# Top-k attention and a SoLU block on one Trainium2 core: the places of the work in a step are changed, and they rank work for a scheduler where they were the order on four engines

## The chip, the cores and the metric

One NeuronCore of a Trainium2 chip runs the whole program. Its engines run their own queues in order and wait for each other through semaphores: PE (TensorE, matmuls and transposes), DVE (VectorE), ACT (ScalarE), POOL (GpSimd), and SP, which here issues all DMA transfers. The metric is the device time of one execution in microseconds (us). Less is better.

## The reference, cut to what matters

```python
# q, k, v: (8, 8, 576, 64)  batch, heads, sequence, head size
scores = scale * q @ k.T                      # 576 x 576 for each head
kth = 32nd largest score of each row
attn = softmax of the row over the scores >= kth, 0 elsewhere
x = attn @ v                                  # as (4608 tokens, 512)
h = x @ w_in                                  # (4608, 1024)
solu = h * softmax(h)
ln = (solu - mean) / sqrt(var + 1e-6) * g_ln
out = ln @ w_out                              # (4608, 512)
```

The MoE weights w_in, w_out and g_ln arrive as 64-bit floats and are converted on the chip.

## The kernel before

The work is cut into 32 pairs (a batch and two of its heads, 9 row tiles of 128 x 576 scores each) and 36 token tiles of 128 tokens. A pair goes through these functions, in this order of dependence:

- `prep_t`, `prep_m`, `moments`, `spread` (PE, with ACT copies `prep_tc` L621, `prep_mc` L639 and L643, `moments_c` L660): transposes q and k, and works out a first guess of the 32nd largest score. `spread_v` (DVE, L690 and L693), `spread_r` (DVE, L701), `first_p` (POOL, L706 to L712) and `first` (DVE, L720) finish the guess.
- `scores` (PE, L745), `evac` (ACT, L756: PSUM to the tile X).
- three counts that narrow the threshold, each over the nine row tiles: `count0` (DVE, L764), then `second` (DVE, L772 to L779); `count1` (ACT, L787), then `third` (DVE, L796 to L804); `count2` (ACT, L819).
- `exps` (ACT, L851, three pieces of three row tiles), `side`, `nearest` (DVE, L840 and L844), `kth` (DVE, L857 to L872): the exact threshold; `keep` (DVE, L881) and `inverse` (L889, L892): masked exponentials and the reciprocal of their sum; `norm` (POOL, L896).
- `transpose_p`, `transpose_last` (PE, L907, L927), `copy_p`, `copy_last` (ACT), `attn_v` (PE, L956), `copy_v` (ACT, L966, L968).

A token tile goes through `mm1` (PE, L980), `hmax` (DVE, L989), `hexp` (ACT, L994), `solu` (DVE, L1004), `square` (ACT, L1014), `ln` (POOL, L1020 to L1025), `transpose_ln` (PE, L1032), `copy_ln` (ACT, L1039), `mm2` (PE, L1044) and `store` (ACT, L1051, then the DMA).

Every call of such a function is put on a list with a place, a number that counts from the step of its pair: `at(place, function, ...)`. A step is one pair, `STEP = 38.0`. `pair_times` gives the places of a pair, `token_times` those of a token tile, `batch_times` says in which steps the token tiles of a batch run: one in each step, and in three steps, where the last 64 positions of two batches are ready, two ("double" below). The list is sorted by place and the calls are made in that order. Before the change all this stands inside `manual_schedule` for PE, ACT, DVE and POOL: these engines run the instructions in the order of the calls. SP's queue was left to the scheduler.

Pools with a fixed number of buffers tie the engines together: two PSUM buffers `big` for y_ps, s_ps and h_ps, two `tp` for all transposes, two `o` for om, ot, o_ps and y_t; two SBUF buffers `lnT`, used for the raw weights (w_raw) as well; two `w`.

The 16 weight chunks are converted in three stages on DVE and POOL (`float64_stages`). `weights_step(n)`, four times in a step, opens chunk n and takes every open chunk one stage further.

Of the kernel before, what the change touches and what calls it, by code (L numbers as in the profile page):

```python
# [65 lines left out]
def general_path(  # L66
# [175 lines left out]
    def topk_softmax(i, t):  # L242
        d = st[i]
        d["P", t] = []
        for sb in d.pop(("S", t)):
            cur, e, m = sb, None, None
            for r in range(TOPK // 8):
                m = small.tile([P, 8], F32, tag="m8", name="m8")
                nc.vector.max(m, cur)
                if r == 0:  # L250
# [193 lines left out]
def fast_path(  # L444
# [30 lines left out]
    NP = H // 2  # L475
# [21 lines left out]
    NPAIR = len(pairs)  # L497
# [26 lines left out]
    w_chunks = []  # L524
# [49 lines left out]

# [480 lines left out]
    todo = []  # L1057
    STEP = 38.0

    def at(time, f, *args):  # L1060
        todo.append((time, len(todo), f, args))

    def pair_times(i):
        b = i * STEP
        at(b - 32, load_qk, i)
        at(b + 1, load_v, i)

        at(b - 17.0, prep_t, i)
        at(b - 16.4, prep_m, i, "q")
        at(b - 13.0, prep_tc, i)  # L1070
        at(b - 12.8, prep_mc, i, "q")
        at(b - 12.7, prep_m, i, "k")
        at(b - 12.2, prep_mc, i, "k")
        at(b - 12.1, moments, i)
        at(b - 11.7, moments_c, i)
        at(b - 11.5, spread, i)
        at(b - 10.5, spread_v, i)
        at(b - 9.7, spread_r, i)
        at(b - 9.0, first_p, i)
        at(b - 6.5, first, i)  # L1080

        for t in range(NM + 1):
            at(b - 9.0 + 1.8 * t, scores, i, t)
        for j in range(NT):
            at(b - 7.5 + 0.9 * j, evac, i, j)
            at(b - 2.0 + 0.77 * j, count0, i, j)
            at(b + 6.4 + 0.77 * j, count1, i, j)
            at(b + 17.7 + 0.77 * j + (1.5 if j > 3 else 0), count2, i, j)
        at(b + 5.2, second, i)
        at(b + 14.3, third, i)  # L1090

        b += STEP
        for g, t in enumerate((4.8, 14.6, 16.1)):
            at(b + t, exps, i, g)
            at(b + 6.2 + 4.26 * g, side, i, g)
            at(b + 30.2 + 2.25 * g, inverse, i, g)
        at(b + 23.0, kth, i)
        for j in range(NT):
            at(b + 6.3 + 1.42 * j, nearest, i, j)
            at(b + 27.9 + 0.75 * j, keep, i, j)  # L1100
            at(b + 31.2 + 0.9 * j, norm, i, j)
            at(b + 32.2 + 0.95 * j, transpose_p, i, j)
            at(b + 32.8 + 0.95 * j, copy_p, i, j)
        for part, t in enumerate((35.5, 39.2, 40.5)):
            at(b + t, transpose_last, i, part)
            at(b + t + 0.6, copy_last, i, part)
        for part, t in enumerate((36.8, 40.6, 42.4)):
            at(b + t, attn_v, i, part)
        at(b + 43.0, copy_v, i, 1)
        at(b + 43.8, copy_v, i, 2)  # L1110

    def token_times(n, x, stores, more=0.0):

        d = {"x": x, "stores": stores}
        late = n > NPAIR
        b = (NPAIR + 1) * STEP + 6.0 + 15.0 * (n - NPAIR - 1) if late else n * STEP + more
        at(b + 6.5, mm1, d)
        at(b + 14.0, hmax, d)
        at(b + 15.4, hexp, d)
        at(b + 17.5, solu, d)  # L1120
        at(b + 20.5, square, d)
        at(b + 22.0, ln, d)
        lt, c = (28.7, 30.0) if late else (27.2, STEP + 13.7 - more / 2)
        for g in range(2):
            at(b + lt + 0.3 * g, transpose_ln, d, g)
            at(b + lt + 0.6 + 0.4 * g, copy_ln, d, g)
        at(b + c, mm2, d)
        at(b + c + 7.3, store, d)

    def batch_times(b):  # L1130
        rows = out[b * S : b * S + SM, :].rearrange("(p t) m -> p t m", t=NM)
        n = NP * (b + 1) + 1
# [15 lines left out]

    at(-10.0, load_g)
    at(-14.0, load_w, 0)  # L1150
    for n in range(len(w_chunks) + 2):
        at(11.0 + STEP / 4 * n, weights_step, n)
    for i in range(NPAIR):
        pair_times(i)
    for b in range(B):
        batch_times(b)
    E = mybir.EngineType
    with tc.manual_schedule(engines={E.PE, E.Activation, E.DVE, E.Pool}):
        for _, _, f, args in sorted(todo, key=lambda x: x[:2]):
            f(*args)  # L1160

# [59 lines left out]
```

## Time and profile before

| | |
|---|---|
| runs | 1852.15, 1855.78, 1857.37 us (median 1855.78) |
| the profiled execution | 1855.06 us, its span 1853.2 us |
| PE busy | 1478.1 us (80%) |
| DVE busy | 1258.0 us (68%) |
| ACT busy | 1159.3 us (63%) |
| POOL busy | 554.0 us (30%) |
| TensorE clock granted, mean | 0.821 of full speed |

The span is the time from the first to the last instruction that the profile shows; the execution's own time is 1.9 us longer. No engine is busy all the time, so the busy shares alone do not tell what sets the end: that is read from the chain of waits and from the step. The granted clock has two levels, 1.2 GHz (0.50 in the rows) and 2.4 GHz (1.00).

### The profile page before, as it was taken

To read this page: it belongs to the slowest core of one execution; us is meant where nothing else is said; L and a number is where in the kernel's file an instruction comes from. 1 tells how busy PE (TensorE), PEld (TensorE's weight loads), DVE (VectorE), ACT (ScalarE), POOL (GpSimd) and SP (SyncE) were. 2 spreads that over 40 slices of the span, in tenths; PEclk is the share of its full clock that TensorE was granted. 3 is DMA by queue.
4 is the path that set the end of the run, shared out by engine and by line. 5 is a ranking of instruction groups with operands and counts; after the bars stand their busy time and mean duration, and the time that the engine had idled before them with its cause. 6 is when DMAs were issued, how large, how long until landed. Compare 5 with 4: busy or idle time off the path is not lost.

```text
span 1853.2 us, 21831 instructions
## 1 busy us (share of the span) xinstructions
PE 1478.1 (80%) x7043; PEld 822.0 (44%) x7043; DVE 1258.0 (68%) x2976; ACT 1159.3 (63%) x2398; POOL 554.0 (30%) x613
## 2 busy tenths in 40 slices
PE   5365357988888888888888897988888897888898
PEld 3132234544444444544444444444444454444443
DVE  3667677677777766677777776577777775777611
ACT  5544566666767775676777774677777764677422
POOL 3457542223333212233322222333222323322310
PEclk9665667788878897888888997888889977888899
DMA  2111100011001110101101000111110000100000
GB/s 72 56 48 47 54 23 16 20 26 26 20 27 26 27 26 7 30 21 26 26 26 27 26 14 20 25 26 26 27 27 19 20 20 20 32 13 13 7 12 25
DMA packets 101899, 48.70 MB, mean 26 GB/s; under 512 B 86920, under 2 KB 95120, under 8 KB 101776
## 3 DMA queue, kind: packets, MB, share of 16 engines
q1 hardware_dynamic: 101776, 47.21, 9.5%
q8 instruction: 59, 0.97, 0.2%
q14 instruction: 64, 0.52, 0.1%
HBM read 37.75 MB, written 9.44 MB: 25 GB/s over the span
## 4 chain that ended last, share of the span: by engine, by line
PE 48%; ACT 33%; DVE 11%; POOL 3%; DMA 2%; issue 2%; SPq 0%; DVEq 0%; ACTq 0%; POOLq 0%
PE s_ps L745 15%; ACT junka L787 8%; ACT sg L819 8%; PE om L956 8%; PE tp_p L907 7%; PE h_ps L980 6%; PE o_ps L1044 6%; ACT PT L921 4%; ACT E L851 3%; ACT X L756 3%; DVE E L881 3%; PE tp_pt L927 2%; DVE w L840 2%; DVE w L844 2%; PE tp_ln L1032 2%
## 5 line engine op out<-in xcount | busy, mean ns | idle before, releaser
L745 PE MATMUL s_ps<-qkT 64*128 64x288 f32 (+1 forms) x1280 | 384.4, 607 | 87.9 <-ACT X L756 55.6
L764 DVE TENSOR_SCALAR_CACHE_REDUCE junkv<-X,t 128x576 bf16<-128x576 f32 x288 | 222.9, 808 | 233.0 <-ACT X L756 232.2
L921 ACT COPY PT<-tp_p 128x512 f32<-128x512 f32 x256 | 147.4, 591 | 336.0 <-PE tp_p L907 336.0
L745 PEld LDWEIGHTS s_ps<-qkT 64*128 64x128 f32 (+1 forms) x1280 | 196.2, 255 | 233.0 <-ACT X L756 135.0
L896 POOL TENSOR_SCALAR E<-E,rden 128x576 f32<-128x576 f32 x288 | 272.6, 965 | 16.6 <-DVE rden L892 14.0
L756 ACT ACTIVATE X<-s_ps 128x576 f32<-128x576 f32 x288 | 186.1, 657 | 145.2 <-PE s_ps L745 111.9
L881 DVE SCALAR_TENSOR_TENSOR E<-X,kth,E 128x576 f32<-128x576 f32 x288 | 260.9, 937 | 0.2
L907 PE MATMUL tp_p<-ident,E 128*128 128x128 f32 x1152 | 219.8, 334 | 50.4 <-POOL E L896 35.9
L1044 PE MATMUL o_ps<-w_out,lnT 128*128 128x512 f32 x576 | 253.9, 594 | 1.2 <-ACT lnT L1039 1.2
L840 DVE SCALAR_TENSOR_TENSOR w<-X,al,sg 128x576 f32<-128x576 f32 x288 | 235.1, 816 | 3.4
L980 PE MATMUL h_ps<-w_in,xTm 128*128 128x512 f32 x512 | 228.0, 598 | 0.0
L819 ACT ACTIVATE sg<-X,t 128x576 bf16<-128x576 f32 x288 | 220.4, 773 | 9.6 <-DVE t L804 9.6
L844 DVE MAX8 w<-w 128x8 f32<-128x576 f32 x288 | 219.2, 761 | 9.9
L787 ACT ACTIVATE junka<-X,t 128x576 bf16<-128x576 f32 x288 | 219.1, 766 | 7.5 <-DVE al L828 5.1
L907 PEld LDWEIGHTS tp_p<-ident,E 128*128 128x128 f32 x1152 | 154.3, 168 | 143.8 <-POOL E L896 75.7
L812 POOL TENSOR_SCALAR tt<-t 128x9 f32<-128x9 f32 x32 | 7.0, 219 | 648.7 <-DVE al L828 646.1
L631 PE MATMUL tp_qk<-ident,km 128*128 128x128 f32 x128 | 32.5, 403 | 187.7 <-ACT qkT L621 187.7
L1044 PEld LDWEIGHTS o_ps<-w_out,lnT 128*128 128x128 f32 x576 | 108.8, 190 | 136.5 <-issue 129.9
L851 ACT ACTIVATE E<-X 128x1728 f32<-128x1728 f32 x96 | 156.9, 1639 | 0.0
L980 PEld LDWEIGHTS h_ps<-w_in,xTm 128*128 128x128 f32 x512 | 94.9, 190 | 110.5 <-issue 107.9
L956 PE MATMUL om<-PT,vm 128*64 128x256 f32 x1024 | 124.6, 385 | 0.0
L690 DVE TENSOR_TENSOR yq<-y_ps,qm 128x512 f32<-128x512 f32 x32 | 22.1, 691 | 140.2 <-PE y_ps L672 130.7
(114 smaller groups left out, 1681.7 us busy)
## 6 DMA issues: line engine op xcount, KB each, us to landing
qm<-in_q_dram SPq DMA_DIRECT2D x32, 256.0 KB, 3.4
km<-in_k_dram SPq DMA_DIRECT2D x32, 256.0 KB, 3.4
vm<-in_v_dram SPq DMA_DIRECT2D x32, 256.0 KB, 2.7
out_dram<-osb SPq DMA_DIRECT2D x32, 256.0 KB, 2.3
w_raw<-in_moe_w_in_dram SPq DMA_DIRECT2D x8, 512.0 KB, 3.9
w_raw<-in_moe_w_out_dram SPq DMA_DIRECT2D x8, 512.0 KB, 3.5
qt<-in_q_dram SPq DMA_DIRECT2D x32, 32.0 KB, 2.2
kt<-in_k_dram SPq DMA_DIRECT2D x32, 32.0 KB, 2.8
```

The source lines that it names most:

```text
L745: nc.tensor.matmul(out=s[:, half, 0:SH], lhsT=qkT[hd, 0, qs], rhs=qkT[hd, 1, half * SH : (half + 1) * SH], start=True, stop=True,)
L756: nc.scalar.activation(out=x_of(i, j).rearrange("p (a s) -> p a s", a=2), in_=d.pop(("s", j))[:, :, 0:SH], func=AF.Copy, scale=scale,)
L787: nc.scalar.activation(out=junk, in_=x_of(i, j), func=AF.Sign, scale=-1.0, bias=d["t1"][:, j : j + 1], accum_out=d["n1"][:, j : j + 1],)
L819: nc.scalar.activation(out=d["sg", j], in_=x_of(i, j), func=AF.Sign, scale=-(1.0 + 2.0**-23), bias=d["t2"][:, j : j + 1], accum_out=d["n2" ...
L840: nc.vector.scalar_tensor_tensor(out=w, in0=x_of(i, j), scalar=d["al"][:, j : j + 1], in1=d.pop(("sg", j)), op0=ALU.subtract, op1=ALU.mult,)
L844: nc.vector.max(d["w8"][:, j, :], w)
L881: nc.vector.scalar_tensor_tensor(out=e, in0=x_of(i, j), scalar=d["kth"][:, j : j + 1], in1=e, op0=ALU.is_ge, op1=ALU.mult, accum_out=den_a ...
L896: nc.gpsimd.tensor_scalar(out=e, in0=e, scalar1=st[i]["rden"][:, j : j + 1], scalar2=1.0, op0=ALU.mult, op1=ALU.mult,)
L907: nc.tensor.transpose(tp[:, c, :], p_of(i, j)[:, c * P : (c + 1) * P], ident)
L956: nc.tensor.matmul(out=o[h * D : (h + 1) * D, :], lhsT=vm[:, h, c, :] if c < NM else vt[:, h, :], rhs=rhs[0:ks, c, :], start=(c == 0), sto ...
L980: nc.tensor.matmul(out=h[:, half, :], lhsT=x[:, c, :], rhs=w_in[:, c, half * 512 : (half + 1) * 512], start=(c == 0), stop=(c == NP - 1),)
L1044: nc.tensor.matmul(out=d["o"], lhsT=d["lnT"][:, c, :], rhs=w_out[:, c, :], start=(c == 0), stop=(c == NF - 1),)
```

## The change

The functions compute what they did; the number of instructions on each engine is the same. Three things differ. The frame `manual_schedule` is gone: the list is still walked by place, but an instruction's place now only ranks it, and the scheduler that builds the program sets the order on PE, ACT, DVE and POOL too, instruction by instruction. The places are other numbers. And `weights_step(n)` is called three times for each chunk, so that a chunk's three stages have places 0, 5 and 7.5 behind its start, all ahead of the next chunk's (9.5 on). The token tiles of a batch run one step later against the pairs.

```diff
-    w_open = []
+    w_gen = [finish_w(n) for n in range(len(w_chunks))]
...
-        if n < len(w_chunks):
-            w_open.append(finish_w(n))
-        for g in list(w_open):
-            if next(g, w_open) is w_open:
-                w_open.remove(g)
+        next(w_gen[n], None)
...
-        for g, t in enumerate((4.8, 14.6, 16.1)):
+        for g, t in enumerate((12.0, 14.4, 19.5)):
             at(b + t, exps, i, g)
...
-            at(b + 27.9 + 0.75 * j, keep, i, j)
+            at(b + 25.5 + 0.75 * j, keep, i, j)
...
-        n = NP * (b + 1) + 1
+        n = NP * (b + 1) + 2
...
-    for n in range(len(w_chunks) + 2):
-        at(11.0 + STEP / 4 * n, weights_step, n)
+    for n in range(len(w_chunks)):
+        for t in (0.0, 5.0, 7.5):
+            at(10.0 + STEP / 4 * n + t, weights_step, n)
...
-    E = mybir.EngineType
-    with tc.manual_schedule(engines={E.PE, E.Activation, E.DVE, E.Pool}):
-        for _, _, f, args in sorted(todo, key=lambda x: x[:2]):
-            f(*args)
+    for _, _, f, args in sorted(todo, key=lambda x: x[:2]):
+        f(*args)
```

Three places in the middle of the program show what this makes of the order. Line numbers of the changed kernel are 4 lower. The first is ACT, from the end of a pair's transposes to the square of the token tile. Before (E is `exps`, junka `count1`, sg `count2`, h_ps and solu belong to the token tile):

```order
L851 ACTIVATE E<-X 128x1728
L966 COPY xTm<-om 128x512
L968 COPY xTt<-ot 128x64
L787 ACTIVATE junka,n_5886<-X,t_5884 128x576 x9
L851 ACTIVATE E<-X 128x1728
L994 ACTIVATE e_sb,rs<-h_ps,hmax 128x1024
L851 ACTIVATE E<-X 128x1728
L819 ACTIVATE sg,n_5887<-X,t_5959 128x576 x4
L1014 ACTIVATE e_sb,var<-solu,nmu 128x1024
L1051 COPY osb<-o_ps 128x512
L819 ACTIVATE sg,n_5887<-X,t_5959 128x576 x4
L621 COPY qkT<-tp_t 128x2x64
```

The same place on ACT in the change:

```order
L847 ACTIVATE E<-X 128x1728
L917 COPY PTt<-tp_p 128x512
L929 COPY PTt<-tp_pt 64x128
L783 ACTIVATE junka,n_6245<-X,t_6243 128x576 x5
L962 COPY xTm<-om 128x512
L783 ACTIVATE junka,n_6245<-X,t_6243 128x576
L964 COPY xTt<-ot 128x64
L783 ACTIVATE junka,n_6245<-X,t_6243 128x576 x3
L847 ACTIVATE E<-X 128x1728
L990 ACTIVATE e_sb,rs<-h_ps,hmax 128x1024
L815 ACTIVATE sg,n_6246<-X,t_6310 128x576 x5
L1010 ACTIVATE e_sb,var<-solu,nmu 128x1024
```

Two of the three E now stand ahead of the copies of the last transposes (the first of them five rows above the rows shown, between two PT copies), one stays in front of the token tile's exponential, and the copies of om and ot have moved in among the nine counts. Behind the last row come osb, the two qkT copies, one sg, the third qkT copy, one sg, the copy into mom and the last two sg. In the six steps at and after a double one all nine sg stand ahead of the qkT copies.

The second place is DVE, from the `keep` of one pair to the `nearest` of the next. Before (junkv is `count0`; r, u and t `second`; w and its maximum `nearest`):

```order
L881 SCALAR_TENSOR_TENSOR E,den_all<-X,kth,E 128x576 x2
L889 TENSOR_SCALAR rden<-den_all 128x3
L892 RECIPROCAL rden<-rden 128x3
L764 TENSOR_SCALAR junkv,c_6097<-X,t_6119 128x576 x9
L772 TENSOR_SCALAR r<-c_6097 128x9
L775 RECIPROCAL r<-r 128x9
L777 TENSOR_TENSOR u<-r,tb 128x9
L779 TENSOR_TENSOR t_6299<-u,ta 128x9
L828 SCALAR_TENSOR_TENSOR al<-n_5887,tt 128x3
L840 SCALAR_TENSOR_TENSOR w<-X,al,sg 128x576
```

In the change the same stretch of DVE begins with

```order
L716 TENSOR_TENSOR t_6087<-mean,zs 128x9
L836 SCALAR_TENSOR_TENSOR w<-X,al,sg 128x576
L718 SCALAR_TENSOR_TENSOR ta<-zs,t_6087 128x9
L760 TENSOR_SCALAR junkv,c_6048<-X,t_6087 128x576 x2
L840 MAX w_5886<-w 128x8
L760 TENSOR_SCALAR junkv,c_6048<-X,t_6087 128x576 x2
L836 SCALAR_TENSOR_TENSOR w<-X,al,sg 128x576 x2
L840 MAX w_5886<-w 128x8
L760 TENSOR_SCALAR junkv,c_6048<-X,t_6087 128x576 x2
```

The nine counts of a pair and the nine `nearest` of the pair before it now alternate; `kth` and six of the nine `keep` follow, ahead of the token tile's hmax, and three `keep` behind it. Before, nine `keep` stood ahead of the counts and all `nearest` behind them, three of these behind hmax.

The third place is POOL, around the token tile's `ln`. Before (E is `norm`; var, rstd and solu are `ln`):

```order
L712 TENSOR_SCALAR tb<-zs 128x9
L896 TENSOR_SCALAR E<-E,rden 128x576 x9
L812 TENSOR_SCALAR tt<-t_6374 128x9
L1020 TENSOR_SCALAR var<-var 128x1
L1024 TENSOR_TENSOR rstd<-var,mhalf 128x1
L1025 TENSOR_SCALAR solu<-solu,nmu,rstd 128x1024
```

In the change:

```order
L708 TENSOR_SCALAR tb<-zs 128x9
L892 TENSOR_SCALAR E<-E,rden 128x576 x6
L808 TENSOR_SCALAR tt<-t_6725 128x9
L892 TENSOR_SCALAR E<-E,rden 128x576 x3
L1016 TENSOR_SCALAR var<-var 128x1
L1020 TENSOR_TENSOR rstd<-var,mhalf 128x1
```

The `norm` of a pair are now cut in six and three, and the three stand directly ahead of `ln`; they belong to the pair whose `keep` has just run, and PE transposes their tiles in the step that follows. On PE the pieces in a step are the same ones, and half of `transpose_ln` (four of eight) now stands ahead of `spread`.

## Rows read from the trace of the kernel before

**Rows 1.** The page's first part, busy time of each engine.

```profile
PE 1478.1 (80%) x7043; PEld 822.0 (44%) x7043; DVE 1258.0 (68%) x2976; ACT 1159.3 (63%) x2398; POOL 554.0 (30%) x613
```

**Rows 2.** Timeline of DVE, `spread_r` of six of the 32 pairs: start, duration.

```profile
10.36 0.76 DVE L701 TENSOR_REDUCE ss<-yq 128x9 f32<-128x576 f32 x1
...
94.35 0.74 DVE L701 TENSOR_REDUCE ss<-yq 128x9 f32<-128x576 f32 x1
...
383.55 0.75 DVE L701 TENSOR_REDUCE ss<-yq 128x9 f32<-128x576 f32 x1
...
692.04 0.75 DVE L701 TENSOR_REDUCE ss<-yq 128x9 f32<-128x576 f32 x1
...
808.95 0.75 DVE L701 TENSOR_REDUCE ss<-yq 128x9 f32<-128x576 f32 x1
...
1658.96 0.75 DVE L701 TENSOR_REDUCE ss<-yq 128x9 f32<-128x576 f32 x1
```

**Rows 3.** Chain that ended last, in order of time, 888 to 942 us: start, length.

```profile
887.40 6.07 ACT junka L787 x16
893.47 1.54 ACT E L851
895.00 1.09 ACT e_sb L994 x2
...
900.66 1.13 ACT e_sb L1014 x2
...
907.51 0.42 PE y_ps L672 x8
...
928.33 1.47 PE s_ps L745 x8
...
939.63 2.39 ACT junka L787 x6
```

**Rows 4.** Stretches of 2.5 us: busy time (and count) of each engine, granted clock.

```profile
901.00:903.50 2.50, 0.15 (x2) 0.00 (x0) 2.29 (x8) 2.50 (x6) 1.42 (x3) 1.00 0.20 66
...
906.00:908.50 2.50, 2.17 (x25) 1.58 (x25) 0.55 (x1) 1.46 (x5) 0.00 (x0) 0.50 0.01 2
...
931.00:933.50 2.50, 2.27 (x20) 1.20 (x14) 0.00 (x0) 0.63 (x2) 0.00 (x0) 1.00 0.00 0
```

**Rows 5.** Who waited for whom, whole span: total us, times, longest.

```profile
PE tp_qk L631 <- ACT qkT L621: 187.7, 25, 28.0
...
PE s_ps L745 <- DVE solu L1004: 23.8, 3, 7.9
...
DVE w_tmp L31 <- DMA w_raw<-in_moe_w_out_dram: 24.0, 8, 3.1
```

**Rows 6.** Groups of instructions: busy us, mean ns of one, idle before.

```profile
L764 DVE TENSOR_SCALAR_CACHE_REDUCE junkv<-X,t 128x576 bf16<-128x576 f32 x288 | 222.9, 808 | 233.0 <-ACT X L756 232.2
...
L896 POOL TENSOR_SCALAR E<-E,rden 128x576 f32<-128x576 f32 x288 | 272.6, 965 | 16.6 <-DVE rden L892 14.0
...
L881 DVE SCALAR_TENSOR_TENSOR E<-X,kth,E 128x576 f32<-128x576 f32 x288 | 260.9, 937 | 0.2
...
L840 DVE SCALAR_TENSOR_TENSOR w<-X,al,sg 128x576 f32<-128x576 f32 x288 | 235.1, 816 | 3.4
L980 PE MATMUL h_ps<-w_in,xTm 128*128 128x512 f32 x512 | 228.0, 598 | 0.0
...
L844 DVE MAX8 w<-w 128x8 f32<-128x576 f32 x288 | 219.2, 761 | 9.9
```

**Rows 7.** All groups of instructions, for the token tile: same columns.

```profile
L1004 DVE SCALAR_TENSOR_TENSOR solu<-h_ps,rs,e_sb 128x1024 f32<-128x1024 f32 x36 | 46.2, 1284 | 1.5
L989 DVE TENSOR_REDUCE hmax<-h_ps 128x1 f32<-128x1024 f32 x36 | 44.1, 1225 | 96.1 <-PE h_ps L980 96.1
```

**Rows 8.** One line's instructions: shortest, median and longest ns.

```profile
L881 DVE SCALAR_TENSOR_TENSOR E<-X,kth,E x288: 787/814/1302, 93.3 to 1749.8; 128x576 f32<-128x576 f32 x144
...
L710 POOL TENSOR_TENSOR zs<-zs,phalf x32: 1794/2255/2266, 11.5 to 1660.6; 128x9 f32<-128x9 f32 x32
```

More of the change, by code (lines that the diff above doesn't have):

```diff
@@ L1066, in pair_times @@
         at(b + 1, load_v, i)
[L1068 to L1079, printed above, removed]
+        at(b - 17.2, prep_t, i)
+        at(b - 17.1, prep_m, i, "q")
@@ L1080, in pair_times @@
+        at(b - 16.8, prep_tc, i)
+        at(b - 16.5, prep_mc, i, "q")
+        at(b - 16.4, prep_m, i, "k")
+        at(b - 15.4, prep_mc, i, "k")
+        at(b - 15.3, moments, i)
+        at(b - 14.6, moments_c, i)
+        at(b - 14.2, spread, i)
+        at(b - 13.2, spread_v, i)
+        at(b - 12.4, spread_r, i)
+        at(b - 12.0, first_p, i)
         at(b - 6.5, first, i)
         for t in range(NM + 1):
-            at(b - 9.0 + 1.8 * t, scores, i, t)
+            at(b - 9.6 + 1.6 * t, scores, i, t)
@@ L1084, in pair_times @@
         for j in range(NT):
[L1085 to L1090, printed above, removed]
+            at(b - 8.4 + 0.8 * j, evac, i, j)
+            at(b - 3.5 + 0.77 * j, count0, i, j)
+            at(b + 5.0 + 0.77 * j, count1, i, j)
+            at(b + 16.0 + 0.77 * j + (2.5 if j > 4 else 0), count2, i, j)
@@ L1092, in pair_times @@
+        at(b + 4.0, second, i)
+        at(b + 12.6, third, i)
         b += STEP
-        for g, t in enumerate((4.8, 14.6, 16.1)):
+        for g, t in enumerate((12.0, 14.4, 19.5)):
             at(b + t, exps, i, g)
-            at(b + 6.2 + 4.26 * g, side, i, g)
-            at(b + 30.2 + 2.25 * g, inverse, i, g)
-        at(b + 23.0, kth, i)
+            at(b + 4.9 + 4.26 * g, side, i, g)
+            at(b + 28.0 + 2.3 * g, inverse, i, g)
+        at(b + 22.6, kth, i)
         for j in range(NT):
-            at(b + 6.3 + 1.42 * j, nearest, i, j)
-            at(b + 27.9 + 0.75 * j, keep, i, j)
-            at(b + 31.2 + 0.9 * j, norm, i, j)
-            at(b + 32.2 + 0.95 * j, transpose_p, i, j)
-            at(b + 32.8 + 0.95 * j, copy_p, i, j)
@@ L1104, in pair_times @@
[L1104 removed]
+            at(b + 5.0 + 1.42 * j, nearest, i, j)
+            at(b + 25.5 + 0.75 * j, keep, i, j)
+            at(b + 29.0 + 0.9 * j, norm, i, j)
+            at(b + 30.4 + 0.9 * j, transpose_p, i, j)
+            at(b + 30.9 + 0.9 * j, copy_p, i, j)
+        for part, t in enumerate((33.6, 37.2, 38.0)):
             at(b + t, transpose_last, i, part)
             at(b + t + 0.6, copy_last, i, part)
[L1107 removed]
+        for part, t in enumerate((36.0, 38.4, 40.4)):
@@ L1108, in pair_times @@
             at(b + t, attn_v, i, part)
-        at(b + 43.0, copy_v, i, 1)
-        at(b + 43.8, copy_v, i, 2)
+        at(b + STEP + 8.1, copy_v, i, 1)
+        at(b + STEP + 8.9, copy_v, i, 2)
     def token_times(n, x, stores, more=0.0):
         d = {"x": x, "stores": stores}
[L1115 to L1120, printed above, removed]
@@ L1121, in token_times @@
-        at(b + 20.5, square, d)
-        at(b + 22.0, ln, d)
-        lt, c = (28.7, 30.0) if late else (27.2, STEP + 13.7 - more / 2)
+        late = n > NPAIR + 1
+        b = (NPAIR + 1) * STEP + 10.0 + 15.0 * (n - NPAIR - 2) if late else n * STEP + more
+        at(b + 5.5, mm1, d)
+        at(b + 12.8, hmax, d)
+        at(b + 14.2, hexp, d)
+        at(b + 16.5, solu, d)
+        at(b + 20.0, square, d)
+        at(b + 21.5, ln, d)
+        lt, c = (27.7, 29.0) if late else (25.5, STEP + 12.7 - more / 2)
```

## The prediction, before the result was known

> **What bounds the kernel now.** I read the busy times first: PE is busy for 80% of the span, DVE 68%, ACT 63% [rows 1], so no engine is the bound by itself. Then I cut the span into steps by `spread_r`, which runs once for each pair [rows 2]. From the eighth pair (383.55) to the last (1658.96) there are 24 steps in 1275.4 us. A double step and the one behind it, 692.04 to 808.95, take 116.9 us; there are three such, 350.7 us together, which leaves 924.7 / 18 = 51.4 us for a single step. Ahead of these lie seven steps in 373.2 us (84.0 for the first two, 289.2 for five), and behind the last pair's `spread_r` come 194.2 us.
>
> Inside a step the reader looks at the chain that ended last [rows 3]. It has two halves. From 887.40 to 907.5 ACT works without a pause: nine count1, E, the token tile's exponential, E, nine count2, its square, the small copies. From 907.51 to 939.63 the chain is mostly PE, with a few waits for ACT and POOL. The halves follow each other: count1 needs the last count0, that needs the last scores, and the scores need the qkT copies that stand on ACT behind eight count2. While ACT is in its half PE runs dry: it waits 187.7 us in 25 places for the L621 copy [rows 5], 4.4 us in this step, and in 901 to 903.5 it is busy for 0.15 of 2.5 us [rows 4]. Behind that gap the granted clock falls to 0.50, and is back at 1.00 in 931 to 933.5 only [rows 4]. So most of the scores run at 1.2 GHz.
>
> **The change, by its parts.** *Nothing is added or removed* on any engine; only the order counts, so each term is a step walked along the new order with durations of the rows. Zero is the start of `spread_v`.
>
> DVE first, since `nearest` now stands among the counts. Up to the last of `second` it has nine counts (0.81 each, 7.3), nine subtractions (0.82, 7.3) and eight or nine maxima (0.76, 6.8) [rows 6]. DVE's four big groups take 938.1 of 1258.0 us [rows 1, 6]; the other 319.9 are 10.0 for a pair, of which I put 4 here, 2 on `kth` and `inverse`, 4 behind. `first` waits for POOL's power (2.26) [rows 8], where before keeps lay between; one maximum covers part, and I add 2 (0 at least, 3 at most). So `second` ends at 27.4.
>
> ACT reaches count1 earlier than that if PE is fast, since two E (1.54 each) [rows 3] have moved into the PE half, where ACT has gaps. Nine count1 take 6.8 (16 rows, eight counts, 6.07) [rows 3], with two small copies among them 7.6: 35.0. DVE hides `kth` and six keeps (2 + 5.6) under these. Then third, hmax (1.2) [rows 7] 36.5, the exponential 1.1, five count2 3.8, the square 1.13 [rows 3]: 42.6. From the square's end (901.8) to y_ps (907.51) it took 5.7 with five count2 between; now there are two, 2.3 less: 46.0, and 0.4 to `spread_v`: 46.4.
>
> POOL makes a second path to the same point, for four transposes of ln stand ahead of `spread` on PE, and three norms ahead of `ln` on POOL. From hmax's end 36.5: three keeps 2.8 [rows 6], solu 1.3 [rows 7] and about 0.8 of small work to the last reciprocal, 41.4; three norms 2.9 [rows 6], 44.3; `ln` 2.0 (an estimate: two small parts, and one of 1024 columns where a norm takes 0.97 for 576), 46.3; four transposes and `spread`, 47.5. I take 47.5 with PE at full clock; 46.4 is the lower bound.
>
> With PE at half clock the scores end later. Now it is 22.3 us from y_ps to the end of the last s_ps (928.33 + 1.47) and 9.8 more to the start of count1 [rows 3], when PE goes on to `mm1`. The norms are done a step earlier now, which saves about 2 us of waits, so `mm1` starts at about 30.5, ends 7.1 later (228.0 us for 32 token tiles [rows 6]), and hmax starts at 37.6, not 35.3. That step takes 2.3 more, 49.8. Which clock? At full clock the 22.3 shrink by some 7, so `mm1` ends near 31, ahead of hmax's turn, and `mm2`, as long, near 38; PE then stands until the L621 copy, near 43: a gap like today's, and the clock falls. In the slow step `mm2` ends near 45 and PE hardly stands. I expect the two to alternate: 48.7.
>
> - Single steps: 18 x (51.4 - 48.7) = 49 us less (29 at 49.8, 90 at 46.4).
> - Doubles: today the second token tile's h_ps holds one of two buffers while its solu stands behind six keeps on DVE; the scores wait for solu 23.8 us in three places [rows 5]. In the change solu stands right behind `spread_v`. PE gets 14 us of extra matmuls [rows 6], but should have some 5 us free in each of two steps. All nine count2 stand ahead of the copies in both (2 x 1.5 more). 2 x 48.7 + 3 + 4 for what doesn't fit + 2.6 for the second solu ahead of the scores = 107 against 116.9: 3 x 10 = 30 us less (5 to 45).
> - The first seven steps: a chunk's raw buffer came free just ahead of the next load, and DVE stood 3 us for each of four loads in a step (24.0 us in eight waits for w_out alone) [rows 5]; the new places free it a chunk earlier. Three steps without weights or token tile: no hmax, exponential, square (-3.4), at half clock, 46.4 each, 139. Two with weights: about 53 and 60 (7 us of conversion on DVE, an estimate, and in the first nine keeps of pair 0 ahead of the counts, 7 more), 113. Together 252 against 289.2. The two first: 75 against 84.0. In all 46 less (20 to 70).
> - The end: one more token tile runs behind the last pair, 15 us of matmuls, but attention and the token tiles ahead of it alternate on PE without waits for POOL. I take 5 us less (10 more to 15 less).
>
> The sum is 130 us; the profiled execution of 1855.06 us (0.7 under the median of the runs, 1855.78) becomes 1725.
>
> **A rule against it.** keep reads X and E from SBUF, two inputs, and takes 787 to 1302 ns, 937 in the mean [rows 6, 8]; the subtraction, alike in shape, takes 816. The difference is what norm's neighbourhood costs today. The Trainium skill (GPSIMD Engine Reference, Specifications) says that GpSimd shares its SBUF interfaces with VectorE and contends with DVE instructions that have two SBUF inputs. The trace agrees with it by that spread. By the rule alone, with each of nine keeps at its 1302, DVE and POOL lose 9 x 0.37 = 3.3 us in a step, and the sum is 130 - 24 x 3.3 = 51 us. I stay with the mean, since the same nine norms run beside the same nine keeps as before.
>
> **Rivals.** (1) *The clock doesn't come back early in any step.* PE alternates between pieces of scores and transposes with short waits for ACT's copies between them; today, too, the low clock lasts through the scores [rows 4]. Then all steps take 49.8: singles 29, doubles 3 x 5 = 15, the rest 46: 90 us less, 1765. The Trainium skill (TensorE: Matmul & The Clock Gate, "A second HAM failure mode: psum-queue depth-cycling") tells of PE standing briefly between groups of matmuls so often that its clock swings; no run here shows that for the new order. (2) *Contention or a blocked head of DVE's queue eats the steady gain*: keeps at 1302 [rows 8], or a subtraction that waits for its count2 while counts wait behind it. At 3 us in a step 72 of the 130 are gone: 1797. Against it: the count2 of the pair are done before `spread`, except the last two. (3) *DVE is the only bound*: the clock stays high and the POOL path is short, 46.4: 90 + 45 + 50, 1670. (4) *Slower*: the clock stays low past the scores, through attn_v and `mm1`. `mm1` then takes 14 for 7 and starts later, hmax starts 8 to 10 us later, and a step takes some 57: 24 x 5.5 more, less 46, 1941. It decides when the clock rises later than 31 us behind `spread_v`; today it is back 23 us behind it [rows 3, 4], so it would need gaps in attn_v that nothing here makes.
>
> **How the numbers follow.** The forecast 0.57; rival 1 0.17; rival 2 0.10, of which 0.03 loses the gain of the first steps as well and ends at no change; rival 3 0.08; rival 4 0.08. The likeliest gives 1725, and its own terms span about 1680 to 1765; the range takes in rivals 1 and 2 and part of 3: 1660 to 1800. A measurement of this kernel tells about 0.3% from no change. Faster by over 0.3%: 0.57 + 0.17 + 0.07 + 0.08 = 0.89. Within 0.3%: 0.03. Slower: 0.08.
>
> **What would show it.** Single steps of 46 to 50 us between two `spread_r`; doubles with their successors near 107; the eighth `spread_r` near 337; two E within the PE half; no wait of tp_p for norm, and fewer waits of s_ps for solu; w_tmp no longer waiting for its DMA; the granted clock at 1.00 through the scores in about every other step. Wrong would be: DVE idle long ahead of a subtraction while counts stand behind it, keep nearer 1.3 than 0.9, or the clock low in `mm1`.

## The result and the profile after

The changed kernel takes 1581.37 us (median of four runs, 1580.09 to 1582.09) against 1854.47 us (four runs): a ratio of 0.8526, 95% interval 0.8511 to 0.8541. It is faster, as predicted, but by 273 us where 130 were forecast, and the time lies below the range of 1660 to 1800. The profiled execution took 1580.09 us with a span of 1578.2, at a mean granted clock of 0.888 (0.821 before).

The page of the profile after: busy time, share of the span, number of instructions; then the chain that ended last, by engine. Line numbers behind the weight stages are 4 lower than before.

```profile
PE 1332.5 (84%) x7043; PEld 751.8 (48%) x7043; DVE 1168.7 (74%) x2976; ACT 1144.2 (72%) x2398; POOL 505.4 (32%) x613
...
DVE 36%; PE 27%; ACT 19%; POOL 11%; issue 6%; DMA 0%; SPq 0%; ACTq 0%; POOLq 0%; DVEq 0%
```

All engines were busy for less than 85% of the span. To see where the time went, cut the span again by `spread_r`; this is the timeline of DVE after (start, duration) for the eighth pair, two neighbours in single steps, the end of a double and its successor, and the last pair.

```profile
339.32 0.75 DVE L697 TENSOR_REDUCE ss<-yq 128x9 f32<-128x576 f32 x1
...
732.56 0.74 DVE L697 TENSOR_REDUCE ss<-yq 128x9 f32<-128x576 f32 x1
775.59 0.74 DVE L697 TENSOR_REDUCE ss<-yq 128x9 f32<-128x576 f32 x1
...
992.08 0.75 DVE L697 TENSOR_REDUCE ss<-yq 128x9 f32<-128x576 f32 x1
1039.56 0.75 DVE L697 TENSOR_REDUCE ss<-yq 128x9 f32<-128x576 f32 x1
...
1389.61 0.75 DVE L697 TENSOR_REDUCE ss<-yq 128x9 f32<-128x576 f32 x1
```

Against [rows 2] the 275.0 us of span split into three. Up to the eighth pair: 383.55 to 339.32, 44.2 less (46 predicted). Behind the last: 194.2 to 188.6, 5.6 less (5 predicted). The 24 steps between: 1275.4 to 1050.3, 225.1 less, where 49 + 30 = 79 were predicted. A single step takes 43.0 us (it was 51.4, forecast 48.7), a double and its successor 44.2 + 47.5 = 91.7 (it was 116.9, forecast 107). So the error is in the size of the steady step, single or double.

One steady step after, as it runs round from `spread_v` to `spread_v`; the timeline of all engines, with the idle time ahead of an instruction and its releaser in brackets.

```profile
773.98 0.69 DVE L686 TENSOR_TENSOR yq<-y_ps,qm 128x512 f32<-128x512 f32 x1 [1.56 <-PE y_ps L668]
...
778.55 0.17 DVE L716 TENSOR_TENSOR t<-mean,zs 128x9 f32<-128x9 f32 x1 [1.55 <-POOL zs L706]
...
780.17 0.81 DVE L760 TENSOR_SCALAR_CACHE_REDUCE junkv<-X,t 128x576 bf16<-128x576 f32 x1
...
780.91 0.76 DVE L840 MAX8 w<-w 128x8 f32<-128x576 f32 x1
781.58 0.80 DVE L760 TENSOR_SCALAR_CACHE_REDUCE junkv<-X,t 128x576 bf16<-128x576 f32 x1
...
796.88 0.15 DVE L775 TENSOR_TENSOR t<-u,ta 128x9 f32<-128x9 f32 x1
...
797.13 0.78 ACT L783 ACTIVATE junka<-X,t 128x576 bf16<-128x576 f32 x1 [3.38 <-DVE t L775]
...
805.60 1.21 DVE L985 TENSOR_REDUCE hmax<-h_ps 128x1 f32<-128x1024 f32 x1
...
811.74 1.14 ACT L1010 ACTIVATE e_sb<-solu,nmu 128x1024 f32<-128x1024 f32 x1
...
813.65 1.11 PE L627 MATMUL tp_qk<-ident,km 128*128 128x128 f32 x4 [3.36 <-ACT qkT L617]
...
817.09 0.69 DVE L686 TENSOR_TENSOR yq<-y_ps,qm 128x512 f32<-128x512 f32 x1 [1.63 <-PE y_ps L668]
```

The reader is to see a ring of 43.11 us: `second` ends at 797.03, 23.05 us behind `spread_v`; count1 starts at once; the maximum over h ends at 806.81 (32.83), the square at 812.88 (38.90), and the copies behind it, with POOL's `ln` beside them, let `spread_v` start at 43.11. The stations are the prediction's; the distances are not. Two of them show in how instructions follow each other: the count at 780.17 is listed with 0.81, but the next instruction starts 0.74 later, and the maximum at 780.91 with 0.76 is followed after 0.67.

Groups of instructions after: busy us, mean ns of one, idle before and what ended it.

```profile
L892 POOL TENSOR_SCALAR E<-E,rden 128x576 f32<-128x576 f32 x288 | 227.4, 805 | 746.9 <-ACT xTt L964 424.3 <-DVE rden L888 219.6 <-DVE nmu L1004 79.2
...
L877 DVE SCALAR_TENSOR_TENSOR E<-X,kth,E 128x576 f32<-128x576 f32 x288 | 228.4, 826 | 10.6 <-ACT E L847 6.9 <-DVE kth L868 0.5
...
L760 DVE TENSOR_SCALAR_CACHE_REDUCE junkv<-X,t 128x576 bf16<-128x576 f32 x288 | 222.6, 805 | 0.5 <-ACT X L752 0.5
```

The last row answers to the first of [rows 6]: before, DVE stood 233.0 us ahead of `count0`, nearly all of it waiting for ACT to bring X; now it is 0.5 us. Keep and norm are shorter too, 826 and 805 ns where they were 937 and 965.

### The profile page after: what moved, and what is told of

Its sections match the earlier page's. It is cut to its first block, busy times and chain, and to the rows that moved or that the text cites. A ratio compares the mean times of both kernels' runs of the same rounds, so it can differ in the third digit from the quotient of the medians.

```text
span 1578.2 us, 21450 instructions
## 1 busy us (share of the span) xinstructions
PE 1332.5 (84%) x7043; PEld 751.8 (48%) x7043; DVE 1168.7 (74%) x2976; ACT 1144.2 (72%) x2398; POOL 505.4 (32%) x613
## 4 chain that ended last, share of the span: by engine, by line
DVE 36%; PE 27%; ACT 19%; POOL 11%; issue 6%; DMA 0%; SPq 0%; ACTq 0%; POOLq 0%; DVEq 0%
ACT junka L783 9%; DVE w L836 9%; DVE junkv L760 8%; DVE w L840 8%; PE o_ps L1040 7%; PE h_ps L976 6%; ACT sg L815 4%; PE s_ps L741 4%; POOL zs L706 3%; PE om L952 3%; PE tp_ln L1028 2%; PE tp_p L903 2%; DVE E L877 2%; POOL E L892 2%; POOL w_tmp L43 2%
## 5 line engine op out<-in xcount | busy, mean ns | idle before, releaser
L892 POOL TENSOR_SCALAR E<-E,rden 128x576 f32<-128x576 f32 x288 | 227.4, 805 | 746.9 <-ACT xTt L964 424.3
L741 PE MATMUL s_ps<-qkT 64*128 64x288 f32 (+1 forms) x1280 | 284.5, 504 | 66.2 <-ACT X L752 29.9
L752 ACT ACTIVATE X<-s_ps 128x576 f32<-128x576 f32 x288 | 175.1, 649 | 135.3 <-PE s_ps L741 131.3
L877 DVE SCALAR_TENSOR_TENSOR E<-X,kth,E 128x576 f32<-128x576 f32 x288 | 228.4, 826 | 10.6 <-ACT E L847 6.9
L741 PEld LDWEIGHTS s_ps<-qkT 64*128 64x128 f32 (+1 forms) x1280 | 160.5, 213 | 139.2 <-ACT X L752 53.5
L903 PE MATMUL tp_p<-ident,E 128*128 128x128 f32 x1152 | 183.4, 293 | 16.6 <-POOL E L892 13.7
L903 PEld LDWEIGHTS tp_p<-ident,E 128*128 128x128 f32 x1152 | 130.9, 147 | 101.7 <-issue 46.6
L952 PE MATMUL om<-PT,vm 128*64 128x256 f32 x1024 | 146.4, 387 | 0.0
L824 DVE SCALAR_TENSOR_TENSOR al<-n,tt 128x3 f32<-128x3 f32 x96 | 27.6, 288 | 107.2 <-ACT sg L815 105.8
L985 DVE TENSOR_REDUCE hmax<-h_ps 128x1 f32<-128x1024 f32 x36 | 43.7, 1214 | 72.8 <-PE h_ps L976 72.8
```

Source lines behind the costliest of these rows:

```text
L741: nc.tensor.matmul(out=s[:, half, 0:SH], lhsT=qkT[hd, 0, qs], rhs=qkT[hd, 1, half * SH : (half + 1) * SH], start=True, stop=True,)
L877: nc.vector.scalar_tensor_tensor(out=e, in0=x_of(i, j), scalar=d["kth"][:, j : j + 1], in1=e, op0=ALU.is_ge, op1=ALU.mult, accum_out=den_a ...
L892: nc.gpsimd.tensor_scalar(out=e, in0=e, scalar1=st[i]["rden"][:, j : j + 1], scalar2=1.0, op0=ALU.mult, op1=ALU.mult,)
L903: nc.tensor.transpose(tp[:, c, :], p_of(i, j)[:, c * P : (c + 1) * P], ident)
L952: nc.tensor.matmul(out=o[h * D : (h + 1) * D, :], lhsT=vm[:, h, c, :] if c < NM else vt[:, h, :], rhs=rhs[0:ks, c, :], start=(c == 0), sto ...
```

## The experiments

**What the free order gives, and what the places give.** Two kernels take the change apart:

```diff
# e1_old_places_ranked: the kernel before, without the frame
-    E = mybir.EngineType
-    with tc.manual_schedule(engines={E.PE, E.Activation, E.DVE, E.Pool}):
-        for _, _, f, args in sorted(todo, key=lambda x: x[:2]):
-            f(*args)
+    for _, _, f, args in sorted(todo, key=lambda x: x[:2]):
+        f(*args)
# e2_new_places_fixed: the kernel after, with the frame put back
```

> The old places and the old order of the weight stages, but the fixed order on four engines taken away, so that the places only rank. Theory (ring): a step is the ring spread_v, counts among nearest on DVE, count1, hmax, the exponential, count2, the copies, spread; the scheduler makes nearly the same ring from the old places, with eight count2 ahead of the prep copies where the change has five and one: 43.1 + about 2.3, 45 to 46 us for a single step, and 30 to 40 us more in the first steps with the weights; 1640 to 1690 us. Rival (mended places): the new numbers carry the gain, and the old ones ranked stay at 49 us a step or more, 1780 us or more.

> The new places and the new weight stages, but as a fixed order on the four engines as before. Theory (ring): keep stands ahead of the counts on DVE again and all three E lie in ACT's half, so ACT's half and PE's half follow each other: 49 to 52 us for a single step, 1770 to 1830 us in all, the difference to the kernel before coming from the weights. Rival (mended places): 45 us a step or less, under 1680 us.

Measured: e1 1611.6 us, ratio 0.8713 [0.8687, 0.8739]; e2 1847.7 us, ratio 0.9981 [0.9965, 0.9998]. Without the frame the old places give single steps of 44.5 us; the new places in a fixed order give steps of 49.7 to 54.5. (The profiled execution of e2 was the longest of its nine, 1862.9 us.) The group of `count0` shows the difference; first e1, then e2.

```profile
L764 DVE TENSOR_SCALAR_CACHE_REDUCE junkv<-X,t 128x576 bf16<-128x576 f32 x288 | 224.1, 803 | 0.0
```

```profile
L760 DVE TENSOR_SCALAR_CACHE_REDUCE junkv<-X,t 128x576 bf16<-128x576 f32 x288 | 226.0, 808 | 230.7 <-ACT X L752 230.3
```

With a fixed order, of old or new places, DVE stands 233.0 or 230.7 us ahead of counts whose X is not there yet; without it, with either places, it does not, since subtractions and maxima of the pair before stand there. So some 240 of the 273 us come with the removal of the frame, on the old places; the new places in the fixed order are worth 0.2%. Both expectations missed: e1 was put at 1640 at best, e2 at 1830 at most. The 0.2% hides two sides: in e2's trace the eighth `spread_r` comes at 348.6, 35 us earlier than before, and the 24 steps behind it and the end take 43 us more.

The idle time of DVE is not itself what the step loses. The landmarks of a single step, in us behind the start of its `spread_v` (means of the single steps in each trace):

| | before | e1 | the change |
|---|---|---|---|
| `second` ends | 25.7 | 22.8 | 23.05 |
| count1 starts | 29.5 | 22.9 | 23.1 |
| the maximum over h ends | 37.7 | 31.4 | 32.8 |
| the square ends | 44.7 | 38.0 | 38.9 |
| next `spread_v` | 51.4 | 44.6 | 43.1 |

The idle time is filled with work that stood behind `second`, so `second` ends only 2.6 us earlier. Another 3.8 us go between `second` and count1, where ACT in the fixed order still had an E and two copies to do, which waited for PE. The timeline of ACT before, in a step whose `second` ends at 935.8:

```profile
936.43 1.65 ACT L851 ACTIVATE E<-X 128x1728 f32<-128x1728 f32 x1
938.64 0.59 ACT L966 COPY xTm<-om 128x512 f32<-128x512 f32 x1 [0.57 <-PE om L956]
939.52 0.21 ACT L968 COPY xTt<-ot 128x64 f32<-128x64 f32 x1 [0.29 <-PE ot L956]
939.63 0.78 ACT L787 ACTIVATE junka<-X,t 128x576 bf16<-128x576 f32 x1
```

From the start of count1 to the maximum's end the change takes 1.6 us more than before, and from there round to `spread_v` 3.5 less. That the frame costs this is shown by e1 and e2; which engine's order is worth how much was not tried apart.

**The weight stages and the added step of the token part, each put back.**

```diff
# e5_old_weights
-    for n in range(len(w_chunks)):
-        for t in (0.0, 5.0, 7.5):
-            at(10.0 + STEP / 4 * n + t, weights_step, n)
+    for n in range(len(w_chunks) + 2):
+        at(11.0 + STEP / 4 * n, weights_step, n)   # and w_open as before
# e6_old_lag
-        n = NP * (b + 1) + 2
+        n = NP * (b + 1) + 1
...
-        at(b + STEP + 8.1, copy_v, i, 1)
-        at(b + STEP + 8.9, copy_v, i, 2)
+        at(b + 42.6, copy_v, i, 1)
+        at(b + 43.4, copy_v, i, 2)   # and the late tokens' base as before
```

> The changed kernel with the weight stages of the kernel before (several chunks open at once, one place for all their stages) and everything else as changed. One theory: the stages alone are what made the first steps shorter than with the old places without a fixed order (eighth spread_r at 354.0 there, 339.3 in the change), so the eighth spread_r comes at 348 to 354, the single steps stay at 43.0 and the time is 1590 to 1596 us. The rival: the first steps are shorter because the steps themselves are, and the stages are hidden, so the eighth spread_r stays within 4 us of 339.3 and the time within 4 us of 1581.

> The changed kernel with the token part one step earlier again, as before (token number without the added step, the two copies of the attention's output at 42.6 and 43.4 instead of the next step's 8.1 and 8.9, the last tokens' base as before). In its steady step ACT does the copies behind the first count1 instead of behind the fifth and seventh, and mm1 needs them at once. One theory, that the added step only moves the token behind the step's critical parts: mm1 starts 3.4 us later (behind one count1 and the two copies), the maximum over h 0.4 to 2 us, single steps are 43.5 to 45 us, the end is some 17 us shorter as in the kernel with the old places and no fixed order (171 from the last spread_r against 188.6), together 1572 to 1605. The rival, that mm1's start matters fully to the ring (hmax, the exponential and the prep copies all move with it): single steps 46 us and more, 1630 or more.

Measured: e5 1588.36 us, ratio 0.8576 [0.8562, 0.8591], eighth `spread_r` at 346.2, single steps 43.1. The stages are worth 7 us, less than the 9 to 15 of the first theory and more than the 4 of the rival. e6 1569.08 us, ratio 0.8475 [0.8461, 0.8489]: single steps unchanged at 43.05, and 172.7 us behind the last `spread_r` instead of 188.6. That is below what either theory allowed. `mm1` did not start the expected 3.4 us later: in a single step it starts 20.8 to 21.7 us behind `spread_v` in both kernels, and in e6 it stands 0.72 us in its middle for the copy of om in the step looked at; so the run does not test a late `mm1`. The added step costs 16 us at the end, gives 4 back in the first steps (eighth `spread_r` at 343.4 in e6) and buys nothing in the middle. Taken from e1: 1611.6, some 35 less by the pair's and token's places (the remainder, and what the 24 steps differ by: 1085.0 to 1050.3), 7 less by the weight stages, 12 more by the added step, is the change's 1581.

**Is it the ring?** Two kernels put work on one engine: three of the nine `count0` done twice on DVE, and the q transposes done five times on PE, so that their result does not change.

```diff
# e3_more_counts, in count0
-        nc.vector.tensor_scalar(
+        for _ in range(2 if j > 5 else 1): nc.vector.tensor_scalar(
# e4_pe_filled, in prep_m
-        for c in range(NM):
+        for c in list(range(NM)) * (5 if nm == "q" else 1):
```

> The change with three of the nine count0 of each pair done twice (the same result written again): three more DVE instructions of 0.73 us ahead of second in every step. Theory (ring through DVE): each step is 1.5 to 2.2 us longer, 45 to 70 us in all. Rival (TensorE and its clock set the step): less than 10 us in all, since DVE is busy for 74% only.

> The change with the four transposes of q done five times (the same result written again): 16 more transposes of PE in each step, in the 3.4 us in which PE waits for the prep copies. Theory (ring through DVE): PE has room there; within 12 us of the change, either way, also where the granted clock then stays at 1.00 in more steps. Rival (PE is the bound): 2.2 us more in each step, 70 us. Rival (the clock that falls in this gap costs time): the clock stays up and the time falls by 25 us or more.

Measured: e3 1670.24 us, ratio 0.9030 [0.9003, 0.9056], single steps 46.2 (+3.2, more than either said). e4 1603.84 us, ratio 0.8671 [0.8645, 0.8696], single steps 43.0 to 43.2, unchanged; the 22 us, more than the 12 expected, lie in the doubles (+3.8 each) and in the first steps (eighth `spread_r` at 350.9). The granted clock of e4's single steps is 0.93 to 0.98 (0.89 to 0.94 in the change), and they gain nothing by it. So in a single step PE has room, and DVE has none ahead of `second`. Why 3.2 and not 2.2, three starts of 0.73? The timeline of DVE in e3, with one row of ACT:

```profile
818.51 0.69 DVE L686 TENSOR_TENSOR yq<-y_ps,qm 128x512 f32<-128x512 f32 x1 [1.91 <-PE y_ps L668]
...
843.53 0.15 DVE L775 TENSOR_TENSOR t<-u,ta 128x9 f32<-128x9 f32 x1
...
850.01 1.29 DVE L877 SCALAR_TENSOR_TENSOR E<-X,kth,E 128x576 f32<-128x576 f32 x1
...
851.31 1.22 DVE L877 SCALAR_TENSOR_TENSOR E<-X,kth,E 128x576 f32<-128x576 f32 x1
...
852.55 1.19 DVE L985 TENSOR_REDUCE hmax<-h_ps 128x1 f32<-128x1024 f32 x1
...
855.94 0.78 ACT L815 ACTIVATE sg<-X,t 128x576 bf16<-128x576 f32 x1 [0.96 <-DVE t L800]
...
865.10 0.69 DVE L686 TENSOR_TENSOR yq<-y_ps,qm 128x512 f32<-128x512 f32 x1 [1.91 <-PE y_ps L668]
```

`second` ends 25.2 us behind `spread_v`, 2.1 later than the 23.05 of the change, as three starts say. The rest comes from the order: DVE now has eight keeps ahead of the maximum over h instead of six, the last two at 1.29 and 1.22 us beside norms, which makes its end 0.3 us later behind `second`; and `third` stands behind the maximum instead of ahead of it, so count2 waits 0.96 us for it and the square ends 7.15 us behind the maximum, not 6.07.

**Taking the preparation out of the ring.** If the copies behind the square close the ring, doing them ahead of it must shorten the step. In e7 and e8 all the preparation was ranked earlier; in e9 to e11 only its part on PE and ACT, with `spread_v` where it was. In all five its loads are 6 to 10 earlier.

```diff
# e7_prep_mid (e8_prep_first: 16 instead of 9 earlier)
-        at(b - 17.2, prep_t, i)
+        at(b - 26.2, prep_t, i)
...
-        at(b - 13.2, spread_v, i)
+        at(b - 22.2, spread_v, i)
# e9_prep_spread_out (e10: and e6's edit; e11: and copies and moments at 20.7 to 21.5)
-        at(b - 17.2, prep_t, i)
...
-        at(b - 16.8, prep_tc, i)
...
-        at(b - 15.4, prep_mc, i, "k")
...
-        at(b - 14.2, spread, i)
+        at(b - 25.7, prep_t, i)
...
+        at(b - 25.5, prep_tc, i)
...
+        at(b - 25.0, prep_mc, i, "k")
...
+        at(b - 24.8, spread, i)
```

> The changed kernel with the preparation of the next pair (transposes, copies, moments, spread, up to the power) 9 us earlier in its places and its loads 8 us earlier; in the order the first two prep copies then stand on ACT behind two count2 ahead of the token's exponential, the third right behind it, and spread_v on DVE ahead of the middle of the keeps. The ring theory (spread_v, DVE's long stretch to second, count1, hmax, exponential, square, prep copies, moments, spread_v; 43.05 us long while PE has 36.6 and DVE 35 us of work in it): the square and the copies behind it leave the ring, single steps become 38 to 41 us, the time 1490 to 1550 us. The rival, that PE's order or ACT's is as long by itself and only happens to agree with the ring: single steps within 1 us of 43.05, 1560 to 1605 us. It could also be slower, if count2 now waits behind the exponential.

> The same with the preparation 16 us earlier: in the order two prep copies stand among the count1, the third behind two count2. The ring theory gives the same as for 9 us (38 to 41 us a step, 1490 to 1550) if no other wait comes in; the copies among the count1 add 1.3 us to the stretch between second and the maximum, so the step is up to 1.3 us longer than with 9 us. The rival: within 1 us of 43.05 a step, 1560 to 1605.

Measured: e7 1866.05 us, ratio 1.0073 [1.0056, 1.0089], steps of 54.6; e8 1762.99 us, ratio 0.9538 [0.9505, 0.9571], steps of 49 to 50. Both theories missed; a cause shows in the timeline of DVE in e7:

```profile
1104.26 0.69 DVE L686 TENSOR_TENSOR yq<-y_ps,qm 128x512 f32<-128x512 f32 x1 [4.39 <-PE y_ps L668]
...
1113.28 0.80 DVE L877 SCALAR_TENSOR_TENSOR E<-X,kth,E 128x576 f32<-128x576 f32 x1
...
1121.52 0.80 DVE L760 TENSOR_SCALAR_CACHE_REDUCE junkv<-X,t 128x576 bf16<-128x576 f32 x1
...
1137.51 0.17 DVE L775 TENSOR_TENSOR t<-u,ta 128x9 f32<-128x9 f32 x1
1145.97 0.17 DVE L792 SCALAR_TENSOR_TENSOR step<-n,u 128x9 f32<-128x9 f32 x1 [8.29 <-ACT junka L783]
...
1149.70 1.23 DVE L985 TENSOR_REDUCE hmax<-h_ps 128x1 f32<-128x1024 f32 x1 [3.15 <-PE h_ps L976]
...
1158.86 0.69 DVE L686 TENSOR_TENSOR yq<-y_ps,qm 128x512 f32<-128x512 f32 x1 [4.38 <-PE y_ps L668]
```

All nine keeps went in front of the counts: `second` ends 33.4 us behind `spread_v` instead of 23.05, and then DVE has nothing to do under count1 and waits 8.29 and 3.15 us. In the changed kernel the keeps fill that time. That is 10.4 of the 11.6 us that e7's step is longer.

> The changed kernel with the preparation of the next pair placed so that only its order on PE and ACT moves and the keeps stay ahead of spread_v on DVE: transposes, copies, moments and y_ps 8 to 10 us earlier in their places, spread_v, spread_r and the power where they were. In the order PE does the q transposes behind mm1, one of the eight chunks of mm2, the k transposes and moments, then the rest of mm2 and y_ps; ACT does two prep copies behind its last exps ahead of the token's exponential, the other two right behind it, ahead of the square. The ring theory (the square, the output copy and the prep copies behind them are part of the 43.05 us): spread_v comes 2 to 4 us earlier after second, single steps are 39 to 41.5 us, the time 1500 to 1550 us. The rival, that another engine's own order is as long: single steps 42.5 us or more, 1565 or more; the slow result of the preparation moved 9 us early would then not have been due to the keeps alone.

> The same with the token part one step earlier. The ring theory: the end is 12 to 16 us shorter as without the moved preparation; but mm1 starts 3.4 us later, so that y_ps, which stands behind mm2 on PE, comes later: single steps 40 to 43 us, 1500 to 1570 us. The rival, that PE's order is not in the ring: 12 to 16 us below the kernel with the added step, single steps equal.

> The same as the last, with the copies, moments and y_ps 4 us later in their places than there: the moments then stand behind all of mm2 on PE and their copy behind the square on ACT. The ring theory: spread_v comes up to 1.5 us later than with the earlier places, single steps 0 to 1.5 us longer. The rival: equal within 0.3 us a step.

Measured: e9 1596.53 us, ratio 0.8604 [0.8586, 0.8622]; e10 1588.84, ratio 0.8560 [0.8544, 0.8576]; e11 1578.99, ratio 0.8511 [0.8494, 0.8529]. Half of the single steps come down to 41.0 us in e9, most to between 40.3 and 41.9 in e10, and nearly all to 40.9 in e11, 2.1 less than 43.05: what the ring theory said, near the upper end, and against the rival. The times missed what the ring theory said in e9 and e10: by their ratios e9 is 0.8% of the old time above the change, e10 and e11 0.9% and 0.4% above e6, whose token part they share. Steps around the doubles grew, in e11 to 52.5 + 51.7 + 45.2. The single steps of e11 are not longer than those of e10 but shorter (40.9 against 41.5 in the median), and the whole by 10 us, which neither of its theories had. In the steps of 40.9 and 41.0 of e9 and e11 the granted clock is 1.00 throughout, in those of 41.8 to 42.0 it is 0.96. In the change a step that starts at full clock, just behind a double, takes 42.7; so some 0.4 of the 2.1 may be the clock's, which was not tried apart. What closes the ring in e9 shows in the timeline of PE, in a step of 41.0 us:

```profile
944.27 0.66 PE L627 MATMUL tp_qk<-ident,km 128*128 128x128 f32 x4 [2.67 <-ACT qkT L617]
...
945.25 6.28 PE L1040 MATMUL o_ps<-w_out,lnT 128*128 128x512 f32 x14
951.46 0.30 PE L668 MATMUL y_ps<-mom,qkT 64*128 64x65 bf16 x8
```

y_ps stands behind fourteen matmuls of `mm2` there. To tell whether the doubles must give back what singles gain, e12 and e13 keep the change's places for three or four pairs of each eight and e11's for the others, from pair 13 on (pairs are counted from 0 here; the token part is e6's):

```diff
+        late = i > 12 and i % 8 in (5, 6, 7)      # e13: (5, 6, 7, 0)
...
-        at(b - 25.7, prep_t, i)
+        at(b - (17.2 if late else 25.7), prep_t, i)
```

> The token part one step earlier, and the preparation placed early as in the last run except for the pairs 13 to 15, 21 to 23 and 29 to 31, whose preparation meets the steps with two tokens and keeps the places of the change. If the ring of the single step is what the early places shorten (43.05 to 40.9) and the steps with two tokens lost only through the early places there: some 15 single steps of 40.9 instead of 43.05 give 32 us, the steps with two tokens go back to 44.5 and 47.5, the time is 1535 to 1550 us. The rival, that the early places cost the steps with two tokens what they give to the others because PE has no room over a whole turn of eight steps: 1565 to 1585 us.

> The same with the places of the change for pairs 16 and 24 too. The first theory: 2 us a pair longer than with three, if the step behind the two was already short there, or shorter if it was not: 1535 to 1555 us. The rival: 1565 to 1585 us.

Measured: e12 1540.29 us, ratio 0.8304 [0.8276, 0.8332]; e13 1538.86 us, ratio 0.8294 [0.8266, 0.8321]. The timeline of DVE in e12: a single step, a double and its successor, the last pair.

```profile
507.50 0.74 DVE L697 TENSOR_REDUCE ss<-yq 128x9 f32<-128x576 f32 x1
548.39 0.74 DVE L697 TENSOR_REDUCE ss<-yq 128x9 f32<-128x576 f32 x1
592.80 0.74 DVE L697 TENSOR_REDUCE ss<-yq 128x9 f32<-128x576 f32 x1
640.28 0.75 DVE L697 TENSOR_REDUCE ss<-yq 128x9 f32<-128x576 f32 x1
...
1365.94 0.75 DVE L697 TENSOR_REDUCE ss<-yq 128x9 f32<-128x576 f32 x1
```

40.9 for the single, 44.4 + 47.5 for the double: both gains at once, as the first theory said, so PE's work over eight steps is not what bounds the kernel. e12 and e13 beat the kernels before and after, and by some 30 us e6, from which they differ by the preparation alone; between the two nothing is told apart. What makes the doubles grow under the early places was not settled.

## Why the prediction was wrong

*The bound and the parts.* The step as unit and the ring through `second`, count1, hmax and the square were right. The end came to 5.6 (5 forecast), and its parts too: e6 prices the added token tile at 16 us (15 forecast). That the first steps came to 44.2 (46 forecast) is luck. The two steps with the last weights took 76.6 and 54.0 (113 together forecast), the three behind them 125.3 (139), the two first 65.3 (75), and the first `spread_r` came 7.7 us later than before, which the prediction did not have. Its account, DVE waiting for loads of raw weights, is half borne out: these waits fell from 44.8 us to 10.1, but to 10.5 with the old stages as well (e5), and the stages are worth only 7.

*"So `second` ends at 27.4"* is the step that failed first: it ended at 23.05. The term is mis-sized, and the ring was right: the prediction added durations of rows. Between the `spread_v` of that step and `second` lie nine counts, nine subtractions and nine maxima, and the starts of neighbours are 0.73, 0.73 and 0.67 us apart (medians over the whole trace), not 0.81, 0.82 and 0.76: 2.2 us. The small work took 2.3, not 4; POOL's power 1.81 us, not 2.26, with a wait of 1.55 for the 2 assumed. The Trainium skill (Perfetto Trace Analysis, Optimizing Scalar/DVE Operations) says that the write acknowledgement at the end of a profiled instruction overlaps with the next one; this trace agrees, with 0.07 to 0.09 us for each. It was to be read before too: there counts that follow each other start 0.733 us apart (median of 129).

*The path behind `second`* was sized well: hmax's end came 2.26 us behind the last count1 (1.5 forecast), the square 6.07 behind that (6.1), `spread_v` 4.21 behind the square (3.8). The POOL path to y_ps was to end 1.1 us later than ACT's; the two end together. PE's transposes of ln, ahead of y_ps, waited 0.32 us for ACT's copy in this step, and 0.86 and 0.40 us for POOL's `ln` in the steps before and after it.

*"I expect the two to alternate: 48.7"* failed as well. The windows of 2.5 us of that step show the granted clock in the column ahead of the last two:

```profile
811.00:813.50 2.50, 0.00 (x0) 0.00 (x0) 0.00 (x0) 2.50 (x8) 2.35 (x4) 0.82 0.06 13
813.50:816.00 2.50, 2.04 (x16) 1.54 (x17) 0.58 (x1) 2.50 (x7) 1.76 (x3) 0.50 0.28 105
816.00:818.50 2.50, 2.50 (x20) 1.68 (x20) 1.41 (x5) 2.50 (x9) 0.00 (x0) 0.50 0.52 118
818.50:821.00 2.50, 2.25 (x12) 1.35 (x12) 1.60 (x3) 1.35 (x3) 1.39 (x2) 0.82 0.51 116
821.00:823.50 2.50, 2.50 (x15) 1.60 (x16) 1.84 (x6) 1.64 (x4) 0.83 (x2) 1.00 0.05 12
```

PE stands 3.36 us and the clock is at 1.2 GHz from 812.6 to 819.4; the first scores alone run slow, and `mm1` ends at 802.4, 28.4 us behind `spread_v`, well ahead of hmax's turn. Every single step has such a stretch, of 7 to 10 us; none alternates. A double and the two steps behind it run at full clock nearly throughout (1.00 from 601.0 to 727.3), and the single step among them takes 42.7 us: by that the clock is worth some 0.4 us a step here. The sum from 48.7: 4.4 less to the start of count1 and through it, 1.1 more behind, 1.1 less for POOL and 1.2 less for the alternation make 43.1. The doubles' term rested on 2 x 48.7; at 2 x 43.1 the same 9.6 on top gives 95.8, and 91.7 was measured.

*The rule against it.* Keep came down to 826 ns and norm to 805: what norms and keeps cost each other became less, since they meet less. Before, 113 of the 288 keeps ran nearly whole beside a norm (1.28 us in the median), after, 5; with nothing of POOL beside it a keep takes 0.81 us in both traces. The prediction's reason to stay with the mean, that the same norms run beside the same keeps, did not hold. Where they still meet, a keep takes 1.29 (e3), which agrees with the Trainium skill's (GPSIMD Engine Reference, Specifications) sharing of SBUF between the two engines.

*The rivals.* The clock that never comes back (1765), contention (1797) and the slower case (1941) are out by the rows above. (By the prediction's own terms the doubles of the first gain 3 x 7.7, not 3 x 5, which makes it 1757.) DVE as the only bound (1670) was nearest in kind; it too carried the 27.4. The removal of the frame, worth some 240 us by itself, is in the prediction only as an order to walk along; DVE's 233.0 us ahead of `count0` stood in [rows 6], and it did not name them as what goes.

## What to carry to other kernels

A long idle time ahead of one group, on an engine that has other ready work, can be a sign of what a fixed order costs: here it fell from 233.0 to 0.0 us by leaving the order to a scheduler, with the old numbers, and the kernel got 240 us shorter. It is not the size of the gain; the landmarks of a step tell where that lies. When a step is added up, take the distance between starts of neighbours, not the durations. And look at the order that a new rank produces on the engine of the ring before trusting it: ranking `spread_v` 9 earlier along with the rest moved nine keeps in front of the counts and cost 11.6 us a step, while the same idea without that gained 2.1.

## What was not expected of the hardware

A maximum directly behind the subtraction whose result it reads starts 0.836 us after it (median of 288, before); an independent instruction behind a subtraction starts 0.73 us after it (median, after). Before, all nine pairs of a step stood so; the free order puts other work between most of them, which by these medians is worth about 0.1 us each, an estimate of 0.9 us a step. POOL's power took 2.26 us in the median before and 1.81 after, and before two or three keeps ran beside it in most steps, after none. But single ones took 2.3 us with no keep beside them (the first pair after, three pairs in e9), so the cause is open.
